# A two-layer spectral mixer and MLP: transposes of 128 columns, plain copy of z, statistics one tile ahead, and the interleave of k moved into a PSUM write

## The chip, the cores and the metric

One core of a Trainium2 chip runs the whole kernel in one launch. The metric is device time in microseconds. A profiled execution gives, beside its time, a trace of what each engine did: PE (TensorE; its weight loads are counted apart as PEld), DVE (VectorE), ACT (ScalarE), POOL (GpSimd) and SP, which here only issues transfers.

## The reference

```python
def reference(A_x, A_w_r, A_w_i, B_x, B_w1, B_b1, B_w2, B_b2):
    # S = 2048, D = 576, F = 4608, bf16
    def _A_ref(x, w_r, w_i):                       # spectral mixer
        X = jnp.fft.rfft2(x.astype(jnp.float32), axes=(-2, -1))
        y = jnp.fft.irfft2(X * (w_r + 1j * w_i), s=(S, D), axes=(-2, -1))
        return y.astype(jnp.bfloat16)
    def _B_ref(x, w1, b1, w2, b2):                 # MLP with its own layernorm
        y = _layernorm(x, axis=-1)
        h = _gelu(jnp.einsum("bsd,df->bsf", y, w1) + b1)
        return jnp.einsum("bsf,fd->bsd", h, w2) + b2
    x = A_x
    x = x + _A_ref(_layernorm(x, axis=-1), A_w_r, A_w_i)
    x = x + _B_ref(_layernorm(x, axis=-1), B_w1, B_b1, B_w2, B_b2)
    x = x + _A_ref(_layernorm(x, axis=-1), A_w_r, A_w_i)
    x = x + _B_ref(_layernorm(x, axis=-1), B_w1, B_b1, B_w2, B_b2)
    return x
```

## The kernel before

x lies in SBUF as 16 tiles of 128 rows by 576 columns. A two-dimensional real Fourier transform is done as matrix products: along d (576 values), then along the sequence in two factors, 16 points and 128 points.

The class `SpectralIn` holds the part that is edited. Per tile it does four steps.

- `fold` (L304): DVE adds and subtracts the two halves of the row. The sum (288 values) serves the even frequencies k, the difference the odd ones. The result is `xf`.
- `turn` (L314): PE transposes `xf` in six pieces of 96 columns into a PSUM tile `pt`; ACT copies it to `xT` (L321).
- `dft_d` (L324): six matmuls of 290 columns, three for each half, against the constant `c_fd`, whose entry is 96 x 6 x 290. The output `pz` has the halves o (even, odd k) apart, and inside each half real (145) beside imaginary (145). ACT copies it to `z` with the layernorm's scale (L334), and here the two halves are interleaved: z is written with a step of two elements, so that k stands in order.
- `dft_v` (L341): the 16-point transform, four matmuls of 290 columns (L344 to L347) with the constant `c_k1` as the stationary operand. Their output `py` is copied to `y1`, by ACT (L350) or by DVE (L352), and `exchange` sends it by a DMA on SP's queue to other partitions of the array `v_sb` or `b_sb`.

The layernorm's mean needs no subtraction here; its scale comes from `ln_bn_one` (L265: two bn_stats and one aggregate on DVE) and `ln_scale` (L271: in the first stage a square root on ACT at L277 and a reciprocal on DVE at L280, for two tiles at a time).

The order of instructions on each engine is that in which the program writes them (a manual schedule). There are two places where `SpectralIn` runs.

In layer 0 `run_all` (L354) runs alone at the start of the kernel. In its iteration i it transposes tile i-1, does the 16-point transform of tile i-4, the transform along d of tile i-2, and at the end of the iteration the fold and the statistics of tile i. Meanwhile x is still being loaded (four tiles on SP's queue, the others on POOL's), and further loads are paced by the copies at L321. `keep_busy` fills PE with matmuls on zeros in the first iterations.

For layer 1 the steps are placed inside the MLP of layer 0: `mlp_down` (L652) runs 72 matmuls per tile (L660), and between them, at fixed places, come the previous tile's fold and statistics, turn, dft_d and dft_v. The last tile's steps come after the MLP, from L703, with `keep_busy` between them. There the square root is replaced by arithmetic on DVE (L287 to L295) for all but the last tile.

After each of the two comes `middle`, the 128-point transform, the weights and the way back, which waits for the last exchange; then `SpectralOut` and the MLP. The `Prep` class transposes normalised tiles for the MLP in five pieces of 128 columns (L600), copied by ACT at L602; the last piece repeats 64 columns.

PSUM is used through two pools: `ps_big`, three buffers of two banks, for `pz` and `py`, and `ps_sm`, two buffers, for the transposes.

Of the kernel before, what the change touches and what calls it, by code (L numbers as in the profile page):

```python
# [10 lines left out]
ACT = mybir.ActivationFunctionType  # L11
ALU = mybir.AluOpType
BF16 = mybir.dt.bfloat16
F32 = mybir.dt.float32
# [7 lines left out]
S, D = 2048, 576  # L22
P = 128
NT = 16
DH = D // 2
KH = 145
KP = 2 * KH
# [10 lines left out]
ENGINES = [getattr(mybir.EngineType, n) for n in ("PE", "Activation", "DVE", "Pool")]  # L38


def _fd():
    d = np.arange(DH)[:, None].astype(np.float64)
    j = np.arange(KH)[None, :].astype(np.float64)
    halves = []
    for odd in range(2):
        ang = 2 * np.pi * d * (2 * j + odd) / D
        re, im = np.cos(ang), -np.sin(ang)
        dead = KH - 1 if odd else 0
        re[:, dead] = 0
        im[:, dead] = 0  # L50
        halves.append(np.concatenate([re, im], axis=1).reshape(3, 96, KP))
    return np.concatenate(halves, axis=0).transpose(1, 0, 2)


def _k1():
# [61 lines left out]
def kernel(  # L117
# [12 lines left out]
    nc = tc.nc  # L130
# [5 lines left out]
    persist = ctx.enter_context(tc.tile_pool(name="persist", bufs=1))  # L136
    arena = ctx.enter_context(tc.tile_pool(name="arena", bufs=1))
    shared = ctx.enter_context(tc.tile_pool(name="shared", bufs=1))
    work = ctx.enter_context(tc.tile_pool(name="work", bufs=2))
# [5 lines left out]
    def uid():  # L145
        _n[0] += 1
        return _n[0]

    def big_ps(shape, dtype=F32):
        return ps_big.tile(shape, dtype, tag="big", name=f"psb{uid()}")  # L150

    def sm_ps(shape, dtype=BF16):
        return ps_sm.tile(shape, dtype, tag="sm", name=f"pss{uid()}")
# [13 lines left out]

    x_sb = persist.tile([P, NT, D], BF16, name="x_sb")
    ident = persist.tile([P, P], BF16, name="ident")
    c_fd = persist.tile([96, 6, KP], BF16, name="c_fd")  # L170
    c_k1 = persist.tile([P, 3, P], BF16, name="c_k1")
    c_f2 = persist.tile([P, 16, 3, P], BF16, name="c_f2")
    c_r1 = persist.tile([P, 2, 256], BF16, name="c_r1")
# [14 lines left out]
    order = [t for q in QUADS for t in q]  # L188
# [11 lines left out]
    marks = {}  # L200
# [64 lines left out]
    def ln_bn_one(mv, t):  # L265
        stats = work.tile([P, 2, nc.vector.BN_STATS_DIM], F32, tag="ln_stats")
        for h in range(2):
            nc.vector.bn_stats(out=stats[:, h, :], in_=x_sb[:, t, h * DH : (h + 1) * DH])  # L268
        nc.vector.bn_aggr(out=mv, in_=stats[:])  # L269

    def ln_scale(mv, mlp, sqrt):  # L271

        n = mv.shape[1]
        rs = work.tile([P, n], F32, tag="ln_rs", bufs=4)
        if sqrt:
            sq = work.tile([P, n], F32, tag="ln_v")
            nc.scalar.activation(  # L277
                out=sq[:], in_=mv[:, :, 1], func=ACT.Sqrt, bias=c_eps[:, 1:2] if mlp else c_eps[:, 0:1], scale=(1.0 + EPS) if mlp else 1.0
            )
            nc.vector.reciprocal(out=rs[:], in_=sq[:])  # L280
            return [(mv[:, i, 0:1], rs[:, i : i + 1]) for i in range(n)]

        vv = work.tile([P, n], F32, tag="ln_v")
        hv = work.tile([P, n], F32, tag="ln_hv")
        tt = work.tile([P, n], F32, tag="ln_t")
        sc, add = (1.0 + EPS, EPS * EPS) if mlp else (1.0, EPS)
        nc.vector.tensor_scalar(out=vv[:], in0=mv[:, :, 1], scalar1=sc, scalar2=add, op0=ALU.mult, op1=ALU.add)  # L287
        nc.vector.tensor_scalar(out=hv[:], in0=vv[:], scalar1=-0.5, scalar2=None, op0=ALU.mult)
        nc.vector.tensor_scalar(
            out=rs[:].bitcast(I32), in0=vv[:].bitcast(I32), scalar1=-0.5, scalar2=1597463007.0, op0=ALU.mult, op1=ALU.add  # L290
        )
        for _ in range(3):
            nc.vector.tensor_mul(out=tt[:], in0=rs[:], in1=rs[:])
            nc.vector.tensor_mul(out=tt[:], in0=tt[:], in1=hv[:])
            nc.vector.scalar_tensor_tensor(out=rs[:], in0=tt[:], scalar=1.5, in1=rs[:], op0=ALU.add, op1=ALU.mult)  # L295
        return [(mv[:, i, 0:1], rs[:, i : i + 1]) for i in range(n)]

    class SpectralIn:
# [3 lines left out]
            self.vx, self.st, self.sqrt = vx, {}, sqrt  # L302

        def fold(self, t, odd_engine):  # L304
            xf = work.tile([P, 2, 320], BF16, tag="xn", bufs=3)
            nc.vector.tensor_tensor(out=xf[:, 0, 0:DH], in0=x_sb[:, t, 0:DH], in1=x_sb[:, t, DH:D], op=ALU.add)  # L306
            odd_engine.tensor_tensor(out=xf[:, 1, 0:DH], in0=x_sb[:, t, 0:DH], in1=x_sb[:, t, DH:D], op=ALU.subtract)
            self.st["xf", t] = xf

        def stats(self, tiles):  # L310
# [2 lines left out]

        def turn(self, t):  # L314
            xf = self.st.pop(("xf", t))
            pt = sm_ps([P, 6, P])
            for o in range(2):
                for ci in range(3):
                    nc.tensor.transpose(pt[0:96, 3 * o + ci, :], xf[:, o, 96 * ci : 96 * ci + 96], ident[:])  # L319
            xT = work.tile([96, 6, P], BF16, tag="turn")  # L320
            marks["turn", t] = nc.scalar.copy(out=xT[:], in_=pt[0:96]).ins  # L321
            self.st["xT", t] = xT

        def dft_d(self, t):  # L324
            xT = self.st.pop(("xT", t))
            pz = big_ps([P, 2, 512])
            for o in range(2):
                for ci in range(3):
                    nc.tensor.matmul(  # L329
                        pz[:, o, 0:KP], lhsT=xT[:, 3 * o + ci, :], rhs=c_fd[:, 3 * o + ci, :],  # L330
                        start=(ci == 0), stop=(ci == 2),
                    )
            z = work.tile([P, 2, KP], BF16, tag="z", bufs=3)
            nc.scalar.activation(  # L334
                out=z[:].rearrange("p r (j o) -> p r o j", o=2),
                in_=pz[:, :, 0:KP].rearrange("p o (r j) -> p r o j", r=2),
                func=ACT.Copy, scale=self.st.pop(("rs", t)),
            )
            self.st["z", t] = z

        def dft_v(self, t, on_act):  # L341
            z = self.st.pop(("z", t))
            py = big_ps([P, 2, 512])
            nc.tensor.matmul(py[:, 0, 0:KP], lhsT=c_k1[:, 0, :], rhs=z[:, 0, :], start=True, stop=False)  # L344
            nc.tensor.matmul(py[:, 0, 0:KP], lhsT=c_k1[:, 2, :], rhs=z[:, 1, :], start=False, stop=True)
            nc.tensor.matmul(py[:, 1, 0:KP], lhsT=c_k1[:, 0, :], rhs=z[:, 1, :], start=True, stop=False)
            nc.tensor.matmul(py[:, 1, 0:KP], lhsT=c_k1[:, 1, :], rhs=z[:, 0, :], start=False, stop=True)  # L347
            y1 = work.tile([P, 2, KP], BF16, tag="y1", bufs=5)
            if on_act:
                ins = nc.scalar.copy(out=y1[:], in_=py[:, :, 0:KP]).ins  # L350
            else:
                ins = nc.vector.tensor_copy(out=y1[:], in_=py[:, :, 0:KP]).ins  # L352
            marks["y1", t] = ins
            exchange(self.vx, t, y1[:])  # L354

        def run_all(self, loads):
            for i in range(NT + 4):
                if 0 <= i - 1 < NT:
                    self.turn(order[i - 1])
                if 0 <= i - 4 < NT:  # L360
                    self.dft_v(order[i - 4], on_act=(i % 2 == 0))
                if 0 <= i - 2 < NT:
                    self.dft_d(order[i - 2])
                if i < 4:
                    keep_busy((5, 1, 1, 1)[i])
                if i < NT:
                    t = order[i]
                    self.fold(t, nc.vector)
                    if i % 2 == 0:
                        mv = work.tile([P, 2, nc.vector.BN_AGGR_DIM], F32, tag="ln_mv", bufs=4)  # L370
                    ln_bn_one(mv[:, i % 2, :], t)
                    if i % 2 == 1:
                        for tt, (_, rs) in zip(order[i - 1 : i + 1], ln_scale(mv, False, self.sqrt)):
                            self.st["rs", tt] = rs
                for call in loads.get(i, ()):
                    call()

# [160 lines left out]
    class Prep:  # L538
# [14 lines left out]
        def moments(self):  # L553
            mean = work.tile([P, 4], F32, tag="ln_hv")
            var = work.tile([P, 4], F32, tag="ln_v")
            sq = work.tile([P, 4], F32, tag="ln_t")
            nc.vector.tensor_scalar(out=mean[:], in0=self.s12[:, 0], scalar1=1.0 / D, scalar2=None, op0=ALU.mult)
            nc.vector.tensor_mul(out=sq[:], in0=mean[:], in1=mean[:])
            nc.vector.scalar_tensor_tensor(out=var[:], in0=self.s12[:, 1], scalar=1.0 / D, in1=sq[:], op0=ALU.mult, op1=ALU.subtract)
            self.mean, self.var = mean, var  # L560
# [157 lines left out]
    for n, (kind, j) in enumerate(first[:-3]):  # L718
        i = 1 + max(n - 1, 0)
# [72 lines left out]
```

## Time and profile before

| | |
|---|---|
| median of 3 runs | 771.15 us (770.66 to 772.56) |
| the profiled execution | 772.16 us, its span 770.4 us |
| PE busy | 743.6 us, 97% of the span |
| ACT busy | 341.8 us, 44% |
| DVE busy | 256.9 us, 33% |
| granted TensorE clock | 1.0 |
| bytes moved by DMA | 41.61 MB |

The span is from the first to the last instruction that the profile shows; the time of the execution has some 1.8 us around it. Busy time counts an instruction from its start to its end. Matmuls overlap, so the time that one holds PE is read from the start of one to the start of the next, not from its duration. "idle before" and the name behind the arrow say how long the engine had stood still and what ended that.

### The profile page before, as it was taken

How to read it: one execution, taken by the hardware profiler on the slowest of the kernel's cores; microseconds unless marked ns; L12 is line 12 of the kernel's file. 1: busy time of each engine (PE TensorE's matmuls, PEld its weight loads, DVE VectorE, ACT ScalarE, POOL GpSimd, SP SyncE). 2: the span in 40 equal slices, each digit the busy share in tenths (PEclk: the TensorE clock that was granted, in tenths of full speed). 3: DMA queues.
4: the chain of work that ended last, by engine and by line, in shares of the span. 5: the costliest groups of instructions: out<-in, count | busy, mean ns of one | idle time of the engine just before them, and what ended most of it. 6: DMA issues, size and time to landing. Idle time of an engine off the chain costs nothing. (4 is left out here: it accounts for less than half of the span.)

```text
span 770.4 us, 12539 instructions
## 1 busy us (share of the span) xinstructions
PE 743.6 (97%) x5207; PEld 464.6 (60%) x5207; DVE 256.9 (33%) x843; ACT 341.8 (44%) x561; POOL 39.8 (5%) x75
## 2 busy tenths in 40 slices
PE   8879999999999999999999898999999999999997
PEld 5645744785478547854686565458646854784476
DVE  5855960245024602330133959201400140010011
ACT  6956855324542464236422866641154035204600
POOL 3320011000000000000004000100000000000000
PEclk9999999999999999999999999999999999999999
DMA  7844935000000000000004510620000000000000
GB/s 225 223 129 163 260 97 181 2 16 9 1 9 17 9 1 9 17 9 1 9 11 143 162 48 1 199 77 17 16 0 8 17 9 0 9 16 9 0 17 16
DMA packets 22377, 41.61 MB, mean 54 GB/s; under 512 B 4292, under 2 KB 15376, under 8 KB 22320
## 3 DMA queue, kind: packets, MB, share of 16 engines
q0 software_dynamic: 5696, 22.57, 9.7%
q1 hardware_dynamic: 16224, 17.76, 7.7%
q8 instruction: 41, 0.67, 0.4%
q10 hardware_dynamic: 400, 0.47, 0.2%
q14 instruction: 16, 0.13, 0.1%
HBM read 28.93 MB, written 2.36 MB: 41 GB/s over the span
## 5 line engine op out<-in xcount | busy, mean ns | idle before, releaser
L660 PEld LDWEIGHTS <-h_sb 128*128 128x128 bf16 x2304 | 223.8, 98 | 56.7
L618 PEld LDWEIGHTS <-w_sb 128*128 128x128 bf16 x1152 | 108.7, 98 | 145.8 <-issue 22.6
L590 DVE TENSOR_SCALAR xn<-x_sb,mv,rs 128x576 bf16<-128x576 bf16 x24 | 9.4, 427 | 198.1 <-PE pss_6918 L600 33.8
L268 DVE BATCH_NORM_STATS2 stats<-x_sb 128x6 f32<-128x288 bf16 x112 | 44.7, 440 | 0.0
L626 PEld LDWEIGHTS <-w1r_sb 64*128 64x128 bf16 x288 | 10.2, 94 | 26.0 <-issue 20.3
L656 DVE TENSOR_TENSOR xb<-x_sb,b_bc 128x576 f32<-128x576 bf16 x32 | 24.0, 749 | 0.0
L329 PEld LDWEIGHTS <-xT 96*128 96x128 bf16 x192 | 19.3, 101 | 7.0 <-ACT xT L321 0.7
L593 POOL COPY xn<-xn 128x64 bf16<-128x64 bf16 x24 | 5.8, 253 | 335.7 <-DVE xn L590 335.5
L319 PEld LDWEIGHTS <-xf 128*96 128x96 bf16 x192 | 15.4, 131 | 11.2 <-DVE xf L306 10.6
L428 PEld LDWEIGHTS <-h_sb 128*128 128x128 bf16 x128 | 12.0, 96 | 14.3 <-issue 9.5
L398 PEld LDWEIGHTS <-c_f_80 128*128 128x128 bf16 x128 | 12.3, 97 | 9.4 <-issue 5.1
L668 DVE TENSOR_TENSOR x_sb<-psb_7445,xb 128x576 bf16<-128x576 f32 x1 | 0.8, 758 | 43.6 <-PE psb_7445 L660 43.6
L668 DVE TENSOR_TENSOR x_sb<-psb_4074,xb 128x576 bf16<-128x576 f32 x1 | 0.8, 758 | 41.6 <-PE psb_4074 L660 41.6
L206 PEld LDWEIGHTS <-zeros 128*128 128x128 bf16 x86 | 8.5, 102 | 10.0 <-DVE h_sb L224 1.0
L211 POOL DMA_DIRECT2D h_sb<-in_A_w_r_dram x8 | 6.0, 750 | 133.3 <-issue 103.6
L269 DVE BATCH_NORM_AGGREGATE mv<-stats 128x2 f32<-128x12 f32 x56 | 11.7, 209 | 1.9
L600 PEld LDWEIGHTS <-xn 128*128 128x128 bf16 x160 | 11.5, 98 | 1.4
L632 ACT ACTIVATE h_sb<-psb_5977,b_sb 128x512 bf16<-128x512 f32 x2 | 1.3, 684 | 23.7 <-PE psb_5977 L626 23.7
L632 ACT ACTIVATE h_sb<-psb_7209,b_sb 128x512 bf16<-128x512 f32 x2 | 1.3, 684 | 23.7 <-PE psb_7209 L626 23.7
L632 ACT ACTIVATE h_sb<-psb_6593,b_sb 128x512 bf16<-128x512 f32 x2 | 1.3, 684 | 23.7 <-PE psb_6593 L626 23.7
L548 ACT ACTIVATE h_sb<-x_sb 128x576 bf16<-128x576 bf16 x16 | 11.0, 686 | 0.1
L306 DVE TENSOR_TENSOR xf<-x_sb 128x288 bf16<-128x288 bf16 x32 | 9.6, 299 | 4.1 <-DMA x_sb<-in_A_x_dram 4.1
(1353 smaller groups left out, 1478.4 us busy)
## 6 DMA issues: line engine op xcount, KB each, us to landing
w_sb<-in_B_w_dram SPq DMA_DIRECT2D x16, 288.0 KB
v_sb<-in_B_w_dram POOLq DMA_DIRECT2D x4, 1152.0 KB, 6.6
h_sb<-const_i POOLq DMA_DIRECT2D x8, 384.0 KB, 5.9
shared_1445<-in_B_w_dram POOLq DMA_DIRECT2D x2, 1440.0 KB, 7.3
shared_5356<-in_B_w_dram POOLq DMA_DIRECT2D x2, 1440.0 KB, 7.8
b_sb<-shared_704 SPq DMA_DIRECT2D x16, 145.0 KB
v_sb<-shared_4643 SPq DMA_DIRECT2D x16, 145.0 KB
h_sb<-in_A_w_r_dram POOLq DMA_DIRECT2D x8, 289.0 KB, 4.4
```

The costliest lines, as they stand in the source:

```text
L268: nc.vector.bn_stats(out=stats[:, h, :], in_=x_sb[:, t, h * DH : (h + 1) * DH])
L269: nc.vector.bn_aggr(out=mv, in_=stats[:])
L319: nc.tensor.transpose(pt[0:96, 3 * o + ci, :], xf[:, o, 96 * ci : 96 * ci + 96], ident[:])
L329: nc.tensor.matmul(pz[:, o, 0:KP], lhsT=xT[:, 3 * o + ci, :], rhs=c_fd[:, 3 * o + ci, :], start=(ci == 0), stop=(ci == 2),)
L398: nc.tensor.matmul(px[:, o, 0:KP], lhsT=c_f2[:, e, pl, :], rhs=vx[:, e, ri, :], start=(q == 0), stop=(q == 1))
L428: nc.tensor.matmul(ph[:, o, 0:KP], lhsT=i1[:, n % 4, pl, :], rhs=xp[:, ri, :], start=(q == 0), stop=(q == 1))
L548: nc.scalar.activation(out=at(h_sb, [P, D], 512 * 34), in_=x_sb[:, self.quad[i], :], func=(ACT.Copy, ACT.Square)[k], accum_out=self.s12[:, ...
L600: nc.tensor.transpose(pt[:, ci, :], xn[:, ci * 128 : (ci + 1) * 128], ident[:])
L618: nc.tensor.matmul(ph[:, q, :], lhsT=w1_sb[:, ci, fc * 128 : (fc + 1) * 128], rhs=yT[:, ci, :], start=(first and ci == 0), stop=(not first ...
L626: nc.tensor.matmul(acc[p][:, q, :], lhsT=w1r_sb[rows, p, :], rhs=yT[rows, 4, :], start=first, stop=not first)
L656: nc.vector.tensor_tensor(out=xb[:], in0=xr, in1=b2_bc[:].rearrange("p (h n) -> p h n", h=2), op=ALU.add)
L660: nc.tensor.matmul(po[:, h, 0:DH], lhsT=hts[fc][:, i * 128 : (i + 1) * 128], rhs=w2_chunk(fc)[:, h * DH : (h + 1) * DH], start=(fc == 0), ...
```

## The change

- `xf` becomes one row of 576 values (in a tile of 640), and `turn` transposes it in five pieces of 128 columns, which start at 0, 128, 256, 384 and 448. The third piece holds columns of both halves and is used by both; the fifth overlaps the fourth by 64 columns, whose rows in the constant are zero. `xT` is 128 x 5 x 128 in place of 96 x 6 x 128. `c_fd` becomes 128 x 6 x 290, with zeros in the rows that don't belong to the half.
- `z` is copied in the order of `pz`, with no step.
- `dft_v` reads z as [o, j] for the real and for the imaginary part, two runs of 145 values, and writes them to `py` as (j o): each matmul writes first every second fp32 column of the output, then the others between them. What is in `py` at the end is what was there before.
- `run_all` does the fold at the start of its iteration, behind the transposes of the tile before; on odd iterations the square root and the reciprocal follow at once, and then the 16-point transform's copy. The statistics of tile i+1 come at the end of iteration i (those of tile 0 right behind its fold).

The calls from within the MLP keep their order. The program has 32 transposes and 32 weight loads fewer; the queues of SP and POOL have the same instructions in the same order, and the load of c_fd, on ACT's queue, is larger by a third.

```diff
+CHUNKS = ((0, 0), (128, 0), (256, 0), (384, 0), (448, 64))
+HALF_CHUNKS = ((0, 1, 2), (2, 3, 4))
...
-    c_fd = persist.tile([96, 6, KP], BF16, name="c_fd")
+    c_fd = persist.tile([P, 6, KP], BF16, name="c_fd")
...
         def fold(self, t, odd_engine):
-            xf = work.tile([P, 2, 320], BF16, tag="xn", bufs=3)
-            nc.vector.tensor_tensor(out=xf[:, 0, 0:DH], in0=x_sb[:, t, 0:DH], in1=x_sb[:, t, DH:D], op=ALU.add)
-            odd_engine.tensor_tensor(out=xf[:, 1, 0:DH], in0=x_sb[:, t, 0:DH], in1=x_sb[:, t, DH:D], op=ALU.subtract)
+            xf = work.tile([P, 640], BF16, tag="xn", bufs=3)
+            nc.vector.tensor_tensor(out=xf[:, 0:DH], in0=x_sb[:, t, 0:DH], in1=x_sb[:, t, DH:D], op=ALU.add)
+            odd_engine.tensor_tensor(out=xf[:, DH:D], in0=x_sb[:, t, 0:DH], in1=x_sb[:, t, DH:D], op=ALU.subtract)
...
         def turn(self, t):
-            pt = sm_ps([P, 6, P])
-            for o in range(2):
-                for ci in range(3):
-                    nc.tensor.transpose(pt[0:96, 3 * o + ci, :], xf[:, o, 96 * ci : 96 * ci + 96], ident[:])
-            xT = work.tile([96, 6, P], BF16, tag="turn")
-            marks["turn", t] = nc.scalar.copy(out=xT[:], in_=pt[0:96]).ins
+            pt = sm_ps([P, 5, P])
+            for ci, (start, _) in enumerate(CHUNKS):
+                nc.tensor.transpose(pt[:, ci, :], xf[:, start : start + 128], ident[:])
+            xT = work.tile([P, 5, P], BF16, tag="turn")
+            marks["turn", t] = nc.scalar.copy(out=xT[:], in_=pt[:]).ins
...
         def dft_d(self, t):
-            nc.scalar.activation(
-                out=z[:].rearrange("p r (j o) -> p r o j", o=2),
-                in_=pz[:, :, 0:KP].rearrange("p o (r j) -> p r o j", r=2),
-                func=ACT.Copy, scale=self.st.pop(("rs", t)),
-            )
+            nc.scalar.activation(out=z[:], in_=pz[:, :, 0:KP], func=ACT.Copy, scale=self.st.pop(("rs", t)))
...
         def dft_v(self, t, on_act):
+            zk = z[:].rearrange("p o (r j) -> p r o j", r=2)
             py = big_ps([P, 2, 512])
-            nc.tensor.matmul(py[:, 0, 0:KP], lhsT=c_k1[:, 0, :], rhs=z[:, 0, :], start=True, stop=False)
-            nc.tensor.matmul(py[:, 0, 0:KP], lhsT=c_k1[:, 2, :], rhs=z[:, 1, :], start=False, stop=True)
-            nc.tensor.matmul(py[:, 1, 0:KP], lhsT=c_k1[:, 0, :], rhs=z[:, 1, :], start=True, stop=False)
-            nc.tensor.matmul(py[:, 1, 0:KP], lhsT=c_k1[:, 1, :], rhs=z[:, 0, :], start=False, stop=True)
+            for r, terms in enumerate((((0, 0), (2, 1)), ((0, 1), (1, 0)))):
+                for q, (pl, ri) in enumerate(terms):
+                    nc.tensor.matmul(
+                        py[:, r, 0:KP].rearrange("p (j o) -> p o j", o=2), lhsT=c_k1[:, pl, :], rhs=zk[:, ri], start=(q == 0), stop=(q == 1)
+                    )
...
         def run_all(self, loads):
+            pairs = {}
+            def moments(n):
+                if n % 2 == 0:
+                    pairs[n // 2] = work.tile([P, 2, nc.vector.BN_AGGR_DIM], F32, tag="ln_mv", bufs=4, name=f"mv{uid()}")
+                ln_bn_one(pairs[n // 2][:, n % 2, :], order[n])
             for i in range(NT + 4):
                 if 0 <= i - 1 < NT:
                     self.turn(order[i - 1])
+                if i < NT:
+                    self.fold(order[i], nc.vector)
+                    if i == 0:
+                        moments(0)
+                if i % 2 == 1 and i < NT:
+                    for tt, (_, rs) in zip(order[i - 1 : i + 1], ln_scale(pairs.pop(i // 2), False, self.sqrt)):
+                        self.st["rs", tt] = rs
                 if 0 <= i - 4 < NT:
                     self.dft_v(order[i - 4], on_act=(i % 2 == 0))
                 if 0 <= i - 2 < NT:
                     self.dft_d(order[i - 2])
                 if i < 4:
                     keep_busy((5, 1, 1, 1)[i])
-                if i < NT:
-                    t = order[i]
-                    self.fold(t, nc.vector)
-                    if i % 2 == 0:
-                        mv = work.tile([P, 2, nc.vector.BN_AGGR_DIM], F32, tag="ln_mv", bufs=4)
-                    ln_bn_one(mv[:, i % 2, :], t)
-                    if i % 2 == 1:
-                        for tt, (_, rs) in zip(order[i - 1 : i + 1], ln_scale(mv, False, self.sqrt)):
-                            self.st["rs", tt] = rs
+                if i + 1 < NT:
+                    moments(i + 1)
```

More of the change, by code (lines that the diff above doesn't have):

```diff
@@ L43, in _fd @@
     j = np.arange(KH)[None, :].astype(np.float64)
-    halves = []
-    for odd in range(2):
-        ang = 2 * np.pi * d * (2 * j + odd) / D
+    out = np.zeros((128, 6, KP))
+    for o in range(2):
+        ang = 2 * np.pi * d * (2 * j + o) / D
         re, im = np.cos(ang), -np.sin(ang)
-        dead = KH - 1 if odd else 0
+        dead = KH - 1 if o else 0
         re[:, dead] = 0
         im[:, dead] = 0
-        halves.append(np.concatenate([re, im], axis=1).reshape(3, 96, KP))
-    return np.concatenate(halves, axis=0).transpose(1, 0, 2)
+        m = np.concatenate([re, im], axis=1)
+        for q, ci in enumerate(HALF_CHUNKS[o]):
+            start, fresh = CHUNKS[ci]
+            for row in range(fresh, 128):
+                if o * DH <= start + row < (o + 1) * DH:
+                    out[row, 3 * o + q] = m[start + row - o * DH]
+    return out
 def _k1():
@@ L327, in dft_d @@
             for o in range(2):
-                for ci in range(3):
+                for q, ci in enumerate(HALF_CHUNKS[o]):
                     nc.tensor.matmul(
-                        pz[:, o, 0:KP], lhsT=xT[:, 3 * o + ci, :], rhs=c_fd[:, 3 * o + ci, :],
-                        start=(ci == 0), stop=(ci == 2),
+                        pz[:, o, 0:KP], lhsT=xT[:, ci, :], rhs=c_fd[:, 3 * o + q, :], start=(q == 0), stop=(q == 2),
                     )
             z = work.tile([P, 2, KP], BF16, tag="z", bufs=3)
-            nc.scalar.activation(
-                out=z[:].rearrange("p r (j o) -> p r o j", o=2),
-                in_=pz[:, :, 0:KP].rearrange("p o (r j) -> p r o j", r=2),
-                func=ACT.Copy, scale=self.st.pop(("rs", t)),
-            )
+            nc.scalar.activation(out=z[:], in_=pz[:, :, 0:KP], func=ACT.Copy, scale=self.st.pop(("rs", t)))
             self.st["z", t] = z
```

## The prediction

> **What bounds the kernel now.** I read the page first, then busy times by stretch, then the timeline inside the two stretches in which the edited code runs. Of the page, the span and the engines:
>
> ```profile
> span 770.4 us, 12539 instructions
> PE 743.6 (97%) x5207; PEld 464.6 (60%) x5207; DVE 256.9 (33%) x843; ACT 341.8 (44%) x561; POOL 39.8 (5%) x75
> ```
>
> The 97% is an average. The chain of waits reaches back only to 427.73 us, behind the edited code, so I cut the time before it into stretches. The columns are PE, PEld, DVE, ACT and POOL busy (with counts), clock, DMA share, GB/s:
>
> ```profile
> 13.00:37.00 24.00, 21.39 (x186) 15.21 (x185) 20.48 (x68) 21.69 (x35) 8.25 (x11) 1.00 0.77 203
> ...
> 150.00:250.00 100.00, 100.00 (x735) 66.42 (x733) 34.12 (x140) 39.25 (x60) 0.99 (x4) 1.00 0.04 10
> 250.00:414.00 164.00, 164.00 (x1144) 103.47 (x1142) 45.35 (x191) 68.32 (x105) 5.47 (x10) 1.00 0.07 20
> ```
>
> The edited code runs twice. In the first spectral stage (1 to 43 us) three engines are 85 to 90% busy and take turns. In the layer-0 MLP (15 tiles inside its down products, the 16th alone in a tail, 413.7 to 420 us) PE never stops, so there the matmul slots alone count. One tile on PE, MLP timeline (start, duration):
>
> ```profile
> 155.26 0.29 PE L344 MATMUL psb_1939<-z,c_k_79 128*128 128x290 bf16 x1
> 155.38 0.29 PE L345 MATMUL psb_1939<-z,c_k_79 128*128 128x290 bf16 x1
> 155.51 0.28 PE L346 MATMUL psb_1939<-z,c_k_79 128*128 128x290 bf16 x1
> 155.63 0.28 PE L347 MATMUL psb_1939<-z,c_k_79 128*128 128x290 bf16 x1
> 155.76 1.63 PE L660 MATMUL psb_1822<-shared_1445,h_sb 128*128 128x288 bf16 x12
> ...
> 160.16 0.50 PE L319 MATMUL pss_2011<-ident,xf 128*96 128x128 bf16 x6
> 160.50 1.14 PE L660 MATMUL psb_1962<-v_sb,h_sb 128*128 128x288 bf16 x8
> ```
>
> Starts tell the price, not durations: four 16-point matmuls hold PE from 155.26 to 155.76, 0.125 us each (another tile: 401.47 to 401.96, 0.1225); six transposes hold it from 160.16 to 160.50, 0.057 each. The first stage's middle, DVE and ACT:
>
> ```profile
> 21.19 0.21 DVE L269 BATCH_NORM_AGGREGATE mv<-stats 128x2 f32<-128x12 f32 x1
> 21.43 0.29 ACT L277 ACTIVATE sq<-mv,c_eps 128x2 f32<-128x2 f32 x1 [0.28 <-DVE mv L269]
> 21.63 0.78 ACT L321 COPY xT<-pss_354 96x768 bf16<-96x768 bf16 x1
> 21.76 0.17 DVE L280 RECIPROCAL rs<-sq 128x2 f32<-128x2 f32 x1 [0.36 <-ACT sq L277]
> 21.84 0.29 DVE L306 TENSOR_TENSOR xf<-x_sb 128x288 bf16<-128x288 bf16 x1
> 22.05 0.30 DVE L307 TENSOR_TENSOR xf<-x_sb 128x288 bf16<-128x288 bf16 x1
> 22.18 0.44 PEld L319 LDWEIGHTS <-xf 128*96 128x96 bf16 x6 [0.40 <-DVE xf L306]
> ```
>
> Every second tile ACT waits 0.28 us for the statistics, DVE 0.36 us for the root, and the next fold, and so PE's transposes, come behind both. This ring sets the pace: transposes of tiles 5 and 15 start at 16.18 and 36.86, so a tile takes 20.68 / 10 = 2.07 us.
>
> **What the Trainium skill says.** (1) "PSUM — Partial Sum Buffer", Specifications (TRN2): PSUM lines hold 8 bytes, and a non-contiguous pattern slows matmuls significantly. "Advanced Engine Details and Errata", PSUM Cachelines, adds that every two consecutive elements should be contiguous. Neither gives a factor. No matmul of before writes PSUM with a step, so the trace can't say. (2) "TensorE: Matmul & The Clock Gate", Back-to-back issue gap, prices a warm matmul at N/2.4 + 2.5 ns, 123 ns at 290 columns: the trace's 0.1225 to 0.125 agrees. (3) "ScalarE: Activation LUTs", What ACT_TABLE_LOAD costs: 186 ns + 0.833 ns an element, and 93 ns for a pointer scale. The y copy of 580 (L350) would be 669, measured 637; z (L334) would be 762, measured 918. The stepped bf16 write of z is the visible difference between the two.
>
> **The change part by part.**
>
> *Transposes.* Six of 96 columns become five of 128. An L600 transpose of 128 columns has the same 0.057 us slot (five from 522.23 to 522.50). So PE gains one slot a tile, 0.057 us. The copy shrinks from 768 to 640 columns: L321 takes 777 ns, L602 with 640 columns 692. ACT gains 0.085 a tile. The transform along d keeps its six matmuls of 290 columns; contracting 128 rows in place of 96 I cost at nothing, as L344 with 128 rows and L329 with 96 have one slot (six L329 in 0.75 us). The one cost: c_fd grows by a third, from 326 to 435 KB, at the 283 GB/s of 4 to 8 us an estimated 0.4 us of DMA in 4 to 12 us, where DMA is 94 to 96% busy and x tile 2 is awaited.
>
> *Plain z.* 637 ns of L350 plus the page's 93 for the pointer scale is 730, an estimate; ACT gains 0.19 a tile. Inside the MLP both ACT gains are worth nothing, as PE works on other matmuls meanwhile; in the tail they are on the path.
>
> *Statistics one tile ahead.* Same DVE and ACT rows, other order; the SP and POOL orders are unchanged. In the middle the fold comes ahead of statistics and both waits (0.28, 0.36) should go. What is late next is DVE itself: per pair, from start to start, cast 0.68 (19.23 to 19.91), fold and statistics 2 x 1.47 (17.77 to 19.23), reciprocal 0.10 (21.76 to the fold), 3.72 us or 1.86 a tile. At the start it costs: statistics of tiles 1 and 2 now stand ahead of their folds, and DVE waits for x to land at 5.22 and 8.72. Each fold, and PE's transposes queued behind it, then follows two statistics and an aggregate, 1.0 us later; the delays overlap, so +1.0 once. Bounds: 0 (absorbed, since ACT's copy of tile 1 waits for the table load anyway) to +2 (each tile pays, plus c_fd).
>
> *The interleave into the 16-point output.* Four matmuls a tile write every second fp32. With two fp32 to a line, a step of two touches one line for each value in place of one for two values. Bounds: 1x (the write keeps pace) to 3x (two extra accesses a pair). I take 2x, half rate, an estimate from the line size: 0.245 us a matmul, +0.1225 each, +0.49 a tile.
>
> **The sum at half rate.**
> - MLP, 15 tiles: 15 x (0.49 - 0.057) = +6.5. Nothing hides it.
> - Tail, 16th tile, a serial chain: +0.49 - 0.06 - 0.10 - 0.19 = +0.1.
> - First stage: start +1.0. Middle: PE needs turn 0.42 - 0.06, 16-point 0.50 + 0.49, d transform 0.74, 2.09 a tile against 2.07 now: PE becomes the bound just where the ring was, and ACT's and DVE's relief is worth nothing: about +0.1 over ten tiles. End: the last matmuls stand on the path to the last exchange, +0.5. Together +1.6, bounds 0 and +4.
>
> Total +8.2. The profiled execution took 772.16 us (span 770.4 and 1.8 around it), so 780.4; it stands 1.0 above the median of the runs shown, 771.15, and I state **779.4**.
>
> **Rivals.**
> - *No price for the step (faster).* If PSUM takes a stepped column each PE cycle, the rest remains: MLP -15 x 0.057 = -0.9; tail -0.35; first stage with DVE as bound, 11 tiles x (2.07 - 1.86) = -2.3, +1.0 at the start, -0.3 at the end. Sum -2.8: 768.3. For it: weight loads at L462 read a stepped SBUF operand and still take 98 ns, so a step is not dear everywhere. Against: two pages name just this write. It decides from the slot of the 16-point matmuls: below about 0.165 us (1.35x) the gains outweigh the cost.
> - *Partial price, about 1.35x.* MLP 15 x (0.17 - 0.057) = +1.7, tail -0.2, first stage still DVE-bound, -1.6: about 771, no change.
> - *Heavier, 3x.* PE then sets the first stage too: MLP +13.8, tail +0.6, first stage about +9: 794.
>
> **How the numbers follow.** Half rate 0.72, no price 0.14, partial 0.07, heavier 0.07. A measurement of this kernel can tell about 0.3%, 2.3 us, from no change. No price straddles that line (768.3 against 768.8): 0.11 of it counts as faster, 0.03 as same; of the partial case 0.05 is same, 0.02 either side; half rate and heavier are slower. That makes faster 0.12, same 0.08, slower 0.80. Half rate alone spans 777 to 783 with the bounds of the first stage; the range reaches down to the no-price case, 768 to 784, and leaves out the heavy case and the tails.
>
> **What would show it.** Right: four 16-point matmuls of an MLP tile holding PE for about 0.98 us, transposes for 0.29, z near 0.73 and xT near 0.69 us, L280 no longer waiting for the root in the middle, fold 2 about 1 us later, PE over 95% busy between 16 and 37 us. The MLP stretch must lengthen by 6 to 7 us, nearly all of the loss. Wrong: a 16-point slot still at 0.125 us; then the kernel is at or below its old time, and only the first stage moved.

## The result, and the profile after

| | before | after |
|---|---|---|
| median of 4 runs | 770.96 us (770.66 to 772.56) | 778.26 us (777.95 to 780.07) |
| ratio of after to before | | 1.0095 (1.0074 to 1.0116) |
| the profiled execution | 772.16 us, span 770.4 | 780.07 us, span 778.3 |

The change makes the kernel 7.3 us slower. The forecast was 779.4 us, 8.2 us slower. Of the page of the changed kernel, the lines that answer to the first two shown of before:

```profile
span 778.3 us, 12437 instructions
PE 751.5 (97%) x5139; PEld 467.5 (60%) x5175; DVE 255.9 (33%) x843; ACT 334.3 (43%) x561; POOL 39.7 (5%) x75
```

ACT is busy 7.5 us less, the relief that the copies of xT and z were to give, and PE 7.9 us more. PE's share of 97% is the same: the share says nothing of the loss, the microseconds do. The busy times by stretch (PE, PEld, DVE, ACT, POOL, clock, DMA share, GB/s), changed kernel:

```profile
13.00:37.00 24.00, 24.00 (x182) 16.95 (x181) 19.27 (x66) 20.09 (x36) 8.22 (x11) 1.00 0.78 218
...
150.00:250.00 100.00, 99.68 (x707) 65.05 (x709) 31.81 (x135) 37.91 (x60) 0.98 (x4) 1.00 0.03 8
```

In the first stage PE went from 21.39 us busy in these 24 to all 24: it is the bound there now. In the MLP it was and is full or nearly so, and does fewer matmuls in the same 100 us (707 for 735). Where they went, the PE timeline of one MLP tile, changed kernel:

```profile
156.12 1.14 PE L352 MATMUL psb_1922<-z,c_k_79 128*128 128x290 bf16 x4
157.06 1.67 PE L674 MATMUL psb_1806<-shared_1429,h_sb 128*128 128x288 bf16 x12
158.57 3.10 PE L674 MATMUL psb_1945<-v_sb,h_sb 128*128 128x288 bf16 x24
161.51 0.44 PE L329 MATMUL pss_1994<-ident,xf 128*128 128x128 bf16 x5
161.79 1.14 PE L674 MATMUL psb_1945<-v_sb,h_sb 128*128 128x288 bf16 x8
```

From the first 16-point matmul to the first L674 of the next output tile (psb_1945) is 156.12 to 158.57, 2.45 us, with twelve L674 between. Before, 155.26 to 157.22, it was 1.96 with the same twelve, up to this line:

```profile
157.22 3.10 PE L660 MATMUL psb_1962<-v_sb,h_sb 128*128 128x288 bf16 x24
```

The difference, 0.49 us, is that of the four matmuls: 0.245 us each in place of 0.1225, if the twelve keep their slot. (The 0.94 us to the first L674 alone reads a little short: the twelve that follow take 1.51 us, and 1.46 before.) The five transposes hold PE for 0.28 us, 161.51 to 161.79, where six held it for 0.34.

The span cut at landmarks of the two traces:

| | before | after | |
|---|---|---|---|
| start to the first 128-point matmul (L398, after: L412) | 46.53 | 46.20 | -0.3 |
| from there to the first tile's addition in the MLP (L668, L682) | 99.65 | 100.90 | +1.2 |
| from the first to the 16th tile's addition | 267.86 | 274.17 | +6.3 |
| tail: from there to the first 128-point matmul of layer 1 | 9.13 | 9.63 | +0.5 |
| from there to the last addition | 343.35 | 343.52 | +0.2 |

The MLP's 6.3 us are the loss: 0.42 a tile. The +1.2 in the second row is none of the change's steps. It lies at the end of the first 128-point stage, where four matmuls take twice their time for some microseconds. PE timeline of the changed kernel, and below it two stretches with all engines (the granted clock is the third figure from the end):

```profile
66.11 0.75 PE L442 MATMUL psb_960<-shared_688,h_sb 128*128 128x290 bf16 x4 [0.67 <-DVE shared_688 L430]
67.29 1.15 PE L442 MATMUL psb_967<-shared_688,h_sb 128*128 128x290 bf16 x4 [0.44 <-DVE shared_688 L430]
68.23 1.17 PE L442 MATMUL psb_974<-shared_688,h_sb 128*128 128x290 bf16 x4
...
68.00:69.00 1.00, 1.00 (x6) 0.59 (x4) 0.00 (x0) 0.52 (x1) 0.00 (x0) 0.50 0.51 158
71.00:72.00 1.00, 1.00 (x6) 0.42 (x5) 0.00 (x0) 0.00 (x0) 0.00 (x0) 1.00 0.47 147
```

These write without a step and are not edited; 0.75 becomes 1.15 because the granted clock was 0.50, by the trace from 67.27 to 70.68 us, after waits of PE for DVE. Such stretches of 3.4 us at half clock are not a price of the step: two experiments without it, statistics alone and pairs, have one at the start of this stage (43.8 to 47.3 and 44.5 to 47.9), which is then about 1 us longer, and the two other kernels with a stepped write have none there (27.0 us). This execution, 780.07 us, is the slowest of the four; the half clock is part of that.

The first stage's middle, timeline of the changed kernel, DVE and ACT:

```profile
22.92 0.21 DVE L280 BATCH_NORM_AGGREGATE mv_346<-stats 128x2 f32<-128x12 f32 x1
23.05 0.25 DVE L317 TENSOR_TENSOR xf<-x_sb 128x288 bf16<-128x288 bf16 x1
23.07 0.68 ACT L331 COPY xT<-pss_385 128x640 bf16<-128x640 bf16 x1
...
23.64 0.31 ACT L288 ACTIVATE sq<-mv_346,c_eps 128x2 f32<-128x2 f32 x1
23.98 0.17 DVE L291 RECIPROCAL rs<-sq 128x2 f32<-128x2 f32 x1 [0.46 <-ACT sq L288]
...
24.11 0.39 PEld L329 LDWEIGHTS <-xf 128*128 128x128 bf16 x5
24.24 0.44 PE L329 MATMUL pss_423<-ident,xf 128*128 128x128 bf16 x5
24.43 0.74 ACT L343 ACTIVATE z<-psb_408,rs 128x580 bf16<-128x580 f32 x1 [0.48 <-PE psb_408 L339]
```

ACT no longer waits for the statistics, and the transposes at 24.24 no longer wait for the fold, which was ready at 23.5: those two waits of the ring are gone. DVE still waits 0.46 us for the root, but the fold now stands ahead of that wait, so nothing follows from it. In their place stands the last line's wait: ACT waits for PE. Tile after tile the transposes start 2.00 or 2.01 us apart (16.21 to 36.27 for ten).

### The profile page after: what moved, and what is told of

Read it like the earlier page. It is cut to its first block, busy times and chain, and to the rows that moved or that the text cites. A ratio compares the mean times of both kernels' runs of the same rounds, so it can differ in the third digit from the quotient of the medians.

```text
span 778.3 us, 12437 instructions
## 1 busy us (share of the span) xinstructions
PE 751.5 (97%) x5139; PEld 467.5 (60%) x5175; DVE 255.9 (33%) x843; ACT 334.3 (43%) x561; POOL 39.7 (5%) x75
## 5 line engine op out<-in xcount | busy, mean ns | idle before, releaser
L674 PEld LDWEIGHTS <-h_sb 128*128 128x128 bf16 x2304 | 225.1, 98 | 59.1
L339 PEld LDWEIGHTS <-xT 128*128 128x128 bf16 x192 | 20.4, 107 | 8.2 <-ACT xT L331 0.5
L352 PEld LDWEIGHTS <-c_k_79 128*128 128x128 bf16 x128 | 14.7, 119 | 8.3 <-issue 0.5
L412 PEld LDWEIGHTS <-c_f_80 128*128 128x128 bf16 x128 | 12.3, 97 | 9.3 <-issue 5.1
L329 PEld LDWEIGHTS <-xf 128*128 128x128 bf16 x160 | 11.7, 101 | 7.1 <-DVE xf L317 5.1
L217 PEld LDWEIGHTS <-zeros 128*128 128x128 bf16 x86 | 8.8, 105 | 10.8 <-issue 1.6
L682 DVE TENSOR_TENSOR x_sb<-psb_7413,xb 128x576 bf16<-128x576 f32 x1 | 0.8, 758 | 43.6 <-PE psb_7413 L674 43.6
L682 DVE TENSOR_TENSOR x_sb<-psb_4047,xb 128x576 bf16<-128x576 f32 x1 | 0.8, 758 | 42.0 <-PE psb_4047 L674 42.0
L614 PEld LDWEIGHTS <-xn 128*128 128x128 bf16 x160 | 11.5, 98 | 1.4
L305 DVE TENSOR_TENSOR tt<-tt,hv 128x1 f32<-128x1 f32 (+1 forms) x63 | 10.1, 160 | 2.2
```

Of the source, the lines that this page charges most:

```text
L329: nc.tensor.transpose(pt[:, ci, :], xf[:, start : start + 128], ident[:])
L339: nc.tensor.matmul(pz[:, o, 0:KP], lhsT=xT[:, ci, :], rhs=c_fd[:, 3 * o + q, :], start=(q == 0), stop=(q == 2),)
L352: nc.tensor.matmul(py[:, r, 0:KP].rearrange("p (j o) -> p o j", o=2), lhsT=c_k1[:, pl, :], rhs=zk[:, ri], start=(q == 0), stop=(q == 1))
L412: nc.tensor.matmul(px[:, o, 0:KP], lhsT=c_f2[:, e, pl, :], rhs=vx[:, e, ri, :], start=(q == 0), stop=(q == 1))
L614: nc.tensor.transpose(pt[:, ci, :], xn[:, ci * 128 : (ci + 1) * 128], ident[:])
L674: nc.tensor.matmul(po[:, h, 0:DH], lhsT=hts[fc][:, i * 128 : (i + 1) * 128], rhs=w2_chunk(fc)[:, h * DH : (h + 1) * DH], start=(fc == 0), ...
```

## The experiments

I asked which part carries the loss, and whether it is the write, the reading of z in two runs, or the rest. The theory: a PSUM line holds two fp32, a step of two touches a line for each value, and the matmul runs at half rate. Stage lengths are from one profile of each kernel. The medians carry the clock too: beside the first four experiments the kernel before ran 35 times, with a median of 770.6 us for the 21 runs with a mean granted clock of 0.999 or more, and 773.7 for the four at 0.995 or less.

**The stepped write alone.** The kernel before, with the plain copy of z and the new `dft_v`:

```diff
-            nc.scalar.activation(out=z[:].rearrange("p r (j o) -> p r o j", o=2), in_=pz[...], ...)
+            nc.scalar.activation(out=z[:], in_=pz[:, :, 0:KP], ...)
-            nc.tensor.matmul(py[:, 0, 0:KP], ..., rhs=z[:, 0, :], ...)      # and three more
+            nc.tensor.matmul(py[:, r, 0:KP].rearrange("p (j o) -> p o j", o=2), ..., rhs=zk[:, ri], ...)
```

> The kernel before with the plain copy of z and the stepped 16-point write alone. Theory (the step of two fp32 halves the rate of the 16-point matmuls): four of them hold PE for 0.98 us in the MLP, as in the changed kernel, but the transposes stay at 0.34, so 15 MLP tiles are 0.49 longer each, +7.3; the first stage, with six slow transposes (0.42 a tile) still on PE, is bound by PE at 2.14 a tile and loses 1 us; tail +0.3. About +8.6 us against the kernel before, 1 to 2 us slower than the changed kernel. Rival (the loss comes from the new fold and statistics order and the larger constant, not from the write): within 1 us of the kernel before, 16-point slot 0.49.

Measured: 782.64 us, ratio 1.0152 (1.0131 to 1.0174), 11.6 us slower. That is 3 us more than expected. The 15 MLP tiles took 275.08 us, +7.2 (0.48 a tile), as expected. Most of the rest is the first stage, where the forecast of 2.14 us a tile was too low: 23.49 us for ten tiles, 2.35. Two lines of its timeline show why:

```profile
20.95 0.29 ACT L277 ACTIVATE sq<-mv,c_eps 128x2 f32<-128x2 f32 x1 [0.71 <-DVE mv L269]
...
24.48 0.44 PEld L319 LDWEIGHTS <-xf 128*96 128x96 bf16 x6 [0.63 <-DVE xf L306]
```

The first is the wait of ACT for the statistics, the second that of the transposes for the fold. In the old order the ring through statistics, root and fold is still there, with waits of 0.71 and 0.63 us every second tile, and PE's longer slots are added to it instead of taking its place. The write alone costs more than the whole change; the rival falls.

**The transposes alone.** The kernel before with `fold`, `turn`, `_fd` and the loop of `dft_d` of the changed kernel.

> The kernel before with the five transposes of 128 columns alone. Theory: one PE slot of 0.057 us a tile is gained in the MLP, -0.9 us; in the first stage the transposes fall from 0.42 to 0.28 us of PE a tile and the copy from 0.78 to 0.69 of ACT, but the ring through statistics, root and fold sets the pace, so at most -1; tail -0.15. Together -1 to -2 us. Rival (the constant that is a third larger delays x and costs the gain): 0 or slower.

Measured: 770.28 us for 771.01, ratio 0.9982 (0.9967 to 0.9997). The 15 tiles took 266.94 us, -0.92, close to 15 slots of 0.057 (0.86); the middle of the first stage kept its pace (20.59 us for ten tiles), so the ring hides the rest there. There the five transposes hold PE 0.40 us (20.46 to 20.85), not the 0.28 expected, as their weight loads wait for the fold. A gain of 0.2%, or 0.7 us, a little less than the 1 to 2 us expected.

**The statistics order alone.** The kernel before with the new `run_all`.

> The kernel before with the statistics one tile ahead alone. MLP unchanged. Theory: the waits of ACT for the statistics (0.28) and of DVE for the root (0.36) go, the middle of the first stage falls from 2.07 to about 1.86 us a tile where DVE is the bound, -2 us over ten tiles; the start costs between 0 and 1 us. Together -1 to -2 us. Rival (statistics ahead of the folds cost 1 us or more at the start and another wait takes the place of the removed one): 0 to +1 us.

Measured: 771.17 us, ratio 1.0003 (0.9990 to 1.0015): no change. The middle fell from 2.07 to 1.97 us a tile, not to 1.86, as ACT comes near its own limit there (20.4 us busy in the 21 from 13 to 34). The end gave back 0.4 of the 1.0 us that the middle won: from the last tile's transposes to the first 128-point matmul it took 10.1 us, before 9.7. In this profile the rest went to half clock in the stage behind:

```profile
44.00:47.00 3.00, 3.00 (x14) 1.84 (x13) 1.34 (x4) 1.46 (x3) 0.00 (x0) 0.50 0.00 0
```

The waits of this kernel, 13 to 44 us (who waited for whom: total us, times, longest), have two lines on transfers:

```profile
DVE y L352 <- DMA v_sb<-y: 2.6, 1, 2.6
PE psb L405 <- DMA v_sb<-y: 2.5, 1, 2.5
```

The copy of y1 waits until an exchange has landed and left its buffer, and the 128-point matmuls wait for the last exchange. In the first profile of before these waits are 2.4 and 1.7 us.

**All but the stepped write.** The changed kernel with z interleaved in its copy and the old `dft_v`.

> The changed kernel with the interleave put back into the copy of z and the 16-point transform as before: new transposes and statistics order, no stepped PSUM write. Theory (all of the loss is the stepped write): MLP tile 0.06 us shorter than in the kernel before, -0.9; first stage -1.5 to -2.5 with DVE and ACT as bounds at about 1.85 us a tile; tail -0.1. 767.5 to 769 us, faster than the kernel before by 2 to 3.5 us. Rival (the loss lies in the other parts): no faster than the kernel before.

Measured: 770.64 us for 771.01, ratio 0.9992 (0.9979 to 1.0005). The loss is gone with the step: the 15 tiles took 266.94 us. But the expected gain of 2 to 3.5 us did not come, so the second half of my theory falls. A part of what did come seems to go with the clock: among runs with a mean granted clock of 0.999 or more, the medians are 769.7 us (5 runs) and 770.6 (21 of before), too few to be sure. The middle did run at 1.90 us a tile; the end took 11.1 us in place of 9.7, with the same waits, larger:

```profile
DVE y L361 <- DMA v_sb<-y: 3.6, 1, 3.6
...
PE psb L414 <- DMA v_sb<-y: 1.8, 1, 1.8
ACT y L359 <- DMA v_sb<-y: 1.2, 1, 1.2
```

**Interleave moved on to the copy of y1.** The matmuls read z in the same two runs of 145 values as in the changed kernel, but write PSUM without a step:

```diff
-                        py[:, r, 0:KP].rearrange("p (j o) -> p o j", o=2), ..., rhs=zk[:, ri], ...
+                        py[:, r, 0:KP].rearrange("p (o j) -> p o j", o=2), ..., rhs=zk[:, ri], ...
-                ins = nc.scalar.copy(out=y1[:], in_=py[:, :, 0:KP]).ins
+                ins = nc.scalar.copy(out=y1[:].rearrange("p r (j o) -> p r o j", o=2), in_=py[:, :, 0:KP].rearrange("p r (o j) -> p r o j", o=2)).ins
```

> The changed kernel with the interleave moved on into the copy of y1: the 16-point matmuls read z in the same two runs of 145 values, but write PSUM without a step. Theory (the stepped write is slow): slot of the four back at 0.49 us, MLP -0.9 us against the kernel before, about 768 us. Rival (the two runs of 145 bf16 values of the moving operand, one of them starting off a 4-byte boundary, are slow, not the write): slot stays at 0.98 us and the time at 778. The copy of y1 takes 0.8 us in place of 0.64 on ACT; on DVE a little more than 0.76.

Measured: 770.02 us for 771.64, ratio 0.9990 (0.9977 to 1.0003). PE timeline, MLP:

```profile
153.13 0.66 PE L352 MATMUL psb<-z,c_k 128*128 128x290 bf16 x4
153.63 1.63 PE L676 MATMUL psb<-shared,h_sb 128*128 128x288 bf16 x12
```

0.50 us for the four: the two runs of the moving operand cost nothing, the write was the price. The copies of y1 take 0.82 us on ACT and 0.81 on DVE. The time, though, is above the 768 us expected.

**Pairs of fp32.** The changed kernel, but each matmul writes two neighbouring fp32, leaves two out, and so on:

```diff
-                        py[:, r, 0:KP].rearrange("p (j o) -> p o j", o=2), ..., rhs=zk[:, ri], ...
+                        py[:, r, 0:292].rearrange("p (a o b) -> p o a b", o=2, b=2), ..., rhs=z[:, :, 144 * ri : 144 * ri + 146].rearrange("p o (a b) -> p o a b", b=2), ...
```

> The changed kernel, but the 16-point matmuls write pairs of neighbouring fp32 with a gap of two behind each pair, 292 columns in all (z is read in other groups, so the order of y1 is not the transform's). Theory (an 8-byte line that holds two fp32 is the unit: what counts is whether two values in a row fall into one line): slot of the four back near 0.49 us and the time about 769. Rival (any output that is not contiguous halves the rate): slot 0.98 us, time 778.

Measured: 770.48 us for 771.64, ratio 0.9981 (0.9968 to 0.9994). PE timeline, MLP:

```profile
153.41 0.66 PE L351 MATMUL psb<-z,c_k 128*128 128x292 bf16 x4
153.91 1.63 PE L673 MATMUL psb<-shared,h_sb 128*128 128x288 bf16 x12
```

Full rate, though each pass leaves out half of the columns, as in the changed kernel. It is enough that values come two by two in 8 bytes; the rival, any gap, falls. Every pair here starts at an even column; pairs across the border of two 8-byte lines were not run, so that the line, and not just a neighbour, is what counts is not shown.

**A step of four.** The changed kernel, but each matmul writes every fourth fp32, in four passes:

```diff
-                        py[:, r, 0:KP].rearrange("p (j o) -> p o j", o=2), ..., rhs=zk[:, ri], ...
+                        py[:, r, 0:292].rearrange("p (a h o) -> p o h a", o=2, h=2), ..., rhs=z[:, :, 144 * ri : 144 * ri + 146].rearrange("p o (h a) -> p o h a", h=2), ...
```

> The changed kernel, but the 16-point matmuls write with a step of four fp32 (16 bytes), 292 columns in four passes (z is read in other groups, so the order of y1 is not the transform's). Theory (one line touched for each value, however far apart): slot 0.98 us as with a step of two, time about 778. Rival (the price grows with the step): slot well above 1 us, 15 MLP tiles longer by that.

Measured: 778.96 us for 771.64, ratio 1.0101 (1.0079 to 1.0122). PE timeline, MLP:

```profile
155.10 1.15 PE L351 MATMUL psb<-z,c_k 128*128 128x292 bf16 x4
156.04 1.68 PE L673 MATMUL psb<-shared,h_sb 128*128 128x288 bf16 x12
```

0.94 us to the next line, as with a step of two, and 274.27 us for the 15 tiles (274.17 there). The price is half rate, not more for a longer way.

**The kernel before, a second profile.**

> The kernel before, unchanged, for a second profile. Theory: the start of the first stage differs from execution to execution (when PE's matmuls reach full pace, 9.7 or 13.3 us, and when x tile 2 lands), by about 2 us, and with it the length of the stage; the middle keeps its 2.07 us a tile and the end its 9.7 us. If PE warms early here, the first stage ends near 44.5 us. Rival (the first stage of the kernel before is always as long as in its first profile): it ends at 46.5 us.

Measured: 770.47 us, and the first stage ended at 44.45 us, 2.1 earlier than in the first profile. Its ten middle tiles took 20.67 us (first profile 20.68) and the end 9.5; the start made the difference: tile 5's transposes start at 14.26 us in place of 16.18. In this trace the matmuls are at full pace from 10.4 us, in the first from 13.5, and x tile 2 is there at 7.85 us in place of 8.72. That agrees with "TensorE: Matmul & The Clock Gate", Part 1, by which matmuls run at half pace at first and the moment of the release differs from run to run; the page's spread is 500 ns either way, though, and here it is 3.1 us between two executions. The first profile of before and that of the changed kernel both start late (16.18 and 16.21, full pace from 13.5 and 12.7), so those two may be compared, if not to the last half microsecond; the experiments but the one with a step of four start earlier, and I compare their middles and ends alone.

**Eight buffers for y1.** The two kernels with the interleave in z, and with it in y1, with one more edit: `bufs=8` for `y1` in place of 5.

> The new transposes and statistics order with the interleave in z, and eight buffers for y1 in place of five. Theory (what the faster middle gains is given back at the end, where the copies of y1 wait up to 3.6 us for exchanges that have not landed): those waits go and the first stage ends up to 1 us earlier, about 769.5 us. Rival (the transfers themselves are the limit: the exchanges land no sooner, whatever the buffers): waits gone, but the first matmul of the 128-point transform starts no earlier, and the time is that of five buffers.

> The same with the interleave in the copy of y1. Theory: the copies' waits for landed exchanges at the end go, first stage up to 1 us shorter, about 769 us, the fastest of these kernels and below the kernel before. Rival (the transfers are the limit): time as with five buffers.

Measured: 769.96 us (ratio 0.9977, 0.9961 to 0.9992) and 770.59 us (0.9978, 0.9966 to 0.9990) for 772.10. The copies no longer wait for exchanges, but of the first stage's end only part is won: with the interleave in z the last copy starts at 37.96 us, two microseconds sooner than with five buffers (0.4 of that from an earlier start of tile 15), and the 128-point matmuls start at 42.84 for 44.37. With the interleave in y1 the last copy starts at 37.46 us for 40.13, but the 128-point matmuls at 43.54 for 44.53: there the rival, the transfers as the limit, is right for the most part. PE waits for the last exchange all the same (interleave in z):

```profile
42.84 3.43 PE L414 MATMUL psb<-v_sb,c_f 128*128 128x290 bf16 x17 [2.31 <-DMA v_sb<-y]
```

Both kernels are faster than the kernel before by 0.2%, their intervals below 1, and than the changed kernel by some 8 us. Neither is shown to be faster than the transposes alone (0.9982), and the forecast that the one with the interleave in y1 would be the fastest, at 769 us, was wrong. Against their parents with five buffers, 0.9992 and 0.9990, the intervals overlap, so a gain from the buffers alone isn't shown. In the profile with the interleave in z three stretches at half clock (from 43.8, 64.2 and 98.4 us) cost more than the first stage won: from the first 128-point matmul to the first tile's addition it took 102.7 us, before 99.7.

The lengths that these readings rest on, in us:

| | ten middle tiles of the first stage | its end | first 128-point stage | 15 MLP tiles |
|---|---|---|---|---|
| before | 20.68 | 9.7 | 27.0 | 267.86 |
| before, second profile | 20.67 | 9.5 | 27.3 | 267.85 |
| after | 20.06 | 9.9 | 28.2 | 274.17 |
| stepped write alone | 23.49 | 10.1 | 27.0 | 275.08 |
| transposes alone | 20.59 | 9.4 | 27.1 | 266.94 |
| statistics alone | 19.66 | 10.1 | 28.0 | 267.85 |
| interleave in z | 18.97 | 11.1 | 27.0 | 266.94 |
| interleave in y1 | 18.64 | 10.8 | 26.9 | 266.97 |
| pairs | 18.35 | 11.5 | 27.8 | 266.97 |
| step of four | 20.12 | 10.0 | 27.0 | 274.27 |
| interleave in z, eight buffers | 19.00 | 10.0 | 28.3 | 266.95 |
| interleave in y1, eight buffers | 18.73 | 10.9 | 27.5 | 266.97 |

(Middle: transposes of tile 5 to those of tile 15. End: from there to the first 128-point matmul. Third: to the first matmul of `SpectralOut`.)

## Why the prediction was right

- **The write at half rate: right, and the step that decided.** Forecast +0.49 us a tile, measured 0.49 in the MLP timeline of the changed kernel and 0.48 a tile with the write alone. "PSUM — Partial Sum Buffer", Specifications (TRN2), says that any non-contiguous pattern slows matmuls; the pairs show that this is too wide. "Advanced Engine Details and Errata", PSUM Cachelines, repeats that and adds that every two consecutive elements should be contiguous; the pairs bear out this second line.
- **Transposes: right.** -0.057 a tile forecast, -0.06 measured in the MLP (266.94 for 267.86). The copy xT took 0.69 us as read off L602, z 0.744 for an estimate of 0.730. This holds where PE never stops; for the first stage see below.
- **MLP sum: right.** +6.5 forecast, +6.3 measured.
- **Tail: mis-sized a little.** +0.1 forecast, +0.5 measured. Step by step from the last addition, the 16-point transform took +0.48 as forecast, but the shorter copies gave only 0.13 (to the d transform) and 0.08 (z), as the filling matmuls of `keep_busy` stand in PE's way, and the last exchange landed 0.22 later. One such length is no firm number: with a step of four the tail took 9.37 us.
- **First stage: the wrong term.** +1.6 forecast, -0.3 measured, in three terms. Half clock (+1.2, not forecast) and what the tail took beyond its forecast (+0.4) made up for most of this error in the profile; that the sum came out near 8.2 there is to that extent luck. *Start*, +1.0 forecast, +0.03 measured: x tile 2 landed at 8.09 us in place of 8.72 and the fold followed the statistics by 0.98 us as forecast, so the transposes of tile 2 came 0.29 later and those of tile 5 at the same time. But full pace set in at 12.7 us in place of 13.5 here, and as the second profile of before showed, the start moves by 2 us on its own, and what the order costs there is not settled by these runs. *Middle*, +0.1 forecast for ten tiles, -0.6 measured: PE is the bound as forecast, but at 2.006 us a tile, not 2.09. I took one slot of 0.057 off the 0.42 us that six transposes held PE in this stage. But the 0.42 held a wait: with the pace set by the ring, the weight loads of the transposes waited for the fold. Where they didn't wait, six held PE 0.34 (before, 14.12 to 14.46, and every second tile with the write alone). With PE as the bound they no longer wait, and five hold it 0.28 (14.21 to 14.49). *End*, +0.5 forecast, +0.26 measured.
- **The rival without a price of the step** said -2.8 us. The kernels without the step measured 0.4 to 1.6 us below before. Its pace for the middle was right (1.86 us a tile forecast, 1.90 and 1.86 measured); what failed was the step from the middle to the stage: the end, 9.7 us before, grew to 10.8 to 11.1, as copies and matmuls waited for exchanges (3.6 us for the longest with the interleave in z). The chain of the first stage ends in a transfer, and that sum had only engines in it.
- **Removing a wait: half seen.** Of the signs, one failed: DVE still waits for the root in the middle (0.46 us), if to no effect. That the statistics order alone brings nothing was not forecast. Its worth shows only beside the slower write: with the old order the write costs 2.35 us a tile, with the new one, and five transposes, 2.01.
- **Left open:** what sets off the 3.4 us at half clock, at 67 us in the changed kernel and at other times or not at all in other profiles, and how much of the 7.3 us between the medians it carries; by stages the two profiles differ by 7.9, with 1.2 of it there. Also open is what the order of the statistics costs at the start.

## What to carry to other kernels

Where an interleave can sit in a copy on an engine with time to spare or in a matmul's output, put it in the copy: the PSUM writes here that didn't put consecutive fp32 columns two by two into 8 bytes doubled the matmul's time, and where PE never stops each such slot is on the path. If a gap in the output can't be avoided, write in pairs. Before a gain in the middle of a stage is booked, look at what ends the stage: here a transfer did, and with five buffers a middle faster by 1.7 to 2.3 us moved the end of the stage by less than half of that.

## What the runs showed of the hardware

- Four matmuls of 290 columns hold PE 0.50 us when they write contiguous fp32 and also when they write pairs with gaps (292 columns), and 0.94 to 0.98 us when they write single values with a step of 8 or of 16 bytes. The step costs a factor of two, and the longer one no more.
- A moving operand of two runs of 145 bf16 values, starting at an even or an odd element, costs a matmul nothing against one run of 290 (0.50 us for four in both).
- A stepped bf16 write to SBUF costs ACT 0.18 us for 580 values (z 0.92 for 0.74; y1 0.82 for 0.64) and DVE 0.05 (0.81 for 0.76).
- Six transposes of 96 columns hold PE 0.34 us and five of 128 hold it 0.28, in the MLP and in the first stage, where their weight loads needn't wait; where these wait for the fold, six hold it 0.42 (before) and five 0.40 (transposes alone).
- The granted TensorE clock can fall to 0.50 for 3.4 us within an execution, and four unstepped matmuls then take 0.94 us in place of 0.50 (67.29 to 68.23, changed kernel).
- The same kernel's first stage ends at 46.5 or at 44.5 us, by when PE reaches full pace (13.5 or 10.4 us) and when x lands (tile 2 at 8.72 or 7.85); a single profile can't show a change of 1 us there.
